# First row of attention units: the weights' conversion steps stand behind the copies in the iterations that multiply with the values

## The chip, the cores and the metric

The kernel runs on one core of one Trainium2 chip. The metric is the device time of one execution in microseconds (us); a kernel's time is the median of several executions. The engines are TensorE (PE, with its weight loads as PEld), VectorE (DVE), ScalarE (ACT), GpSimd (POOL) and SyncE (SP, which here only issues DMAs).

## What is computed

A thresholded attention over 8 batches and 8 heads (576 tokens, head size 64) is followed by a mixer block over tokens and channels. Cut to what matters:

```python
scores = q @ k.T / 8                          # (8, 8, 576, 576)
thresh = scores.max(-1) - tau
attn = exp(where(scores >= thresh, scores, -1e9) - scores.max(-1))
x = (attn / (attn.sum(-1) + 1e-9)) @ v        # heads side by side: (8, 576, 512)
h = relu(x.T @ w_tok1) @ w_tok2               # 576 -> 256 -> 576, per channel
u = x + h.T
out = u + relu(u @ w_ch1) @ w_ch2             # 512 -> 1536 -> 512
```

The four weights reach the kernel as 64-bit floats and have to be converted to 32 bits on the chip; q, k and v are 32-bit.

## The kernel before, in words

The attention is cut into 144 units of 128 score rows of two heads, 18 units per batch ("row"); a row has two groups of nine units, and one group covers two pairs of heads. A loop over u (line 640 on) is a software pipeline written out by hand: every engine does its instructions in the order in which the loop emits them, and nothing reorders them. For unit u the loop emits:

- scores(u): PE multiplies q with k into PSUM (L304), VectorE takes the row maxima mx (L309), POOL makes the bias from them (L310).
- values that are due (L411 and L416 on PE). In row 0 they come in the iterations u = 5, 8, 11, 14 and 17, which the code calls a visit. Their result pv lies in one of the two buffers of the PSUM pool ps_tr and is copied to xT by VectorE (L423); the copy is put into the list `copies` and emitted later in the same iteration.
- norm(u - 1): VectorE makes the reciprocals of the row sums (L333, L334), POOL multiplies e by them (L337).
- turn(u - 2): nine transposes on PE in three groups (L355); each group has a buffer of ps_tr, and its copy to eT (L357) is VectorE's for the first and the third group, ScalarE's for the second.
- weigh(u): ScalarE computes e by a Prelu from PSUM (L319), then the exponentials with their row sums (L326).
- on some iterations prep: VectorE transposes a loaded q and k (L286), at the end of the iteration before the one that uses them.

Between these lies the conversion of the weights, cut into 31 pieces with four raw buffers. weight(n) emits n steps, and three steps are one piece. Step k is part k mod 3 of piece k div 3. Every step has one VectorE instruction: L207 (part 0), L209 (part 1) and L213 (part 2). Part 0 also emits POOL's integer add that ends the piece before it (L221), and on SP the load of a later piece into the buffer that this add frees (L182); parts 1 and 2 also emit a ScalarE instruction for the next piece (L197 and L199). weight_to(x) goes on until int(x) steps are done. In row 0 an iteration without a visit brings the count to 2.25 (u - 1.5) in its middle and to 2.25 (u - 1) at its end (L706). An iteration with a visit does all of it in the middle, ahead of weigh, the copies and the turns. From row 1 on (u of 18 and above) other lines set the steps.

In row 0 the score tiles rotate over three PSUM buffers, from unit 18 on over two; the mixer's steps (L447 transposes, L454 and L464 token part, L507 and L528 channel part) then fill PE beside the attention of the next row. The channel steps need converted weights.

Of the kernel before, what the change touches and what calls it, by code (L numbers as in the profile page):

```python
# [21 lines left out]
def kernel(  # L22
# [206 lines left out]
    def weight(n):  # L229

        nonlocal steps_done
        for k in range(steps_done, min(steps_done + n, 3 * len(pieces) + 1)):
            i, part = divmod(k, 3)
            if part == 0:
                on_gpsimd(i - 1)
                if i:
                    load_piece(i - 1 + NRAW)
            else:
                on_scalar(i + 1, part - 1)
            on_vector(i, part)  # L240
            steps_done = k + 1

    def weight_to(x):

        weight(max(int(x) - steps_done, 0))
# [31 lines left out]
    def in_blocks(b):  # L277
        return b > 0
# [11 lines left out]
    def scores(u):  # L290
        b, p0, t = units[u]
        sc = [
            (ps_3rd if b == 0 and (2 * u + h) % 3 == 2 else ps_sc).tile([P, 2, MAIN], F32, tag="sc", name=f"sc{h}_{u}") for h in range(2)
        ]
        if t == SHARED:
            parts = [(b * NP + p0, slice(MAIN, S), slice(0, 64)), (b * NP + p0 + 1, slice(0, LAST), slice(64, P))]
        else:
            o = P * t if t < SHARED else LAST + P * (t - SHARED - 1)
            parts = [(b * NP + p0 + (t > SHARED), slice(o, o + P), slice(0, P))]
        order = [(f, part, h) for f in range(2) for part in parts for h in range(2)]  # L300
        for f, (n, cols, rows), h in order if b else sorted(order, key=lambda o: o[2]):
            r = slice(D * h, D * h + D)
            qT, kT = heads[n]
            nc.tensor.matmul(sc[h][rows, f, 0:HS], lhsT=qT[r, cols], rhs=kT[r, HS * f : HS * f + HS], start=True, stop=True)  # L304
        mx = small.tile([P, 2], F32, tag="mx", name=f"mx_{u}")
        bias = small.tile([P, 2], F32, tag="bias", name=f"bias_{u}")
        for h in range(2):
            c = slice(h, h + 1)
            nc.vector.tensor_reduce(out=mx[:, c], in_=sc[h][:, :, 0:HS], axis=AX.XY, op=ALU.max)  # L309
            nc.gpsimd.tensor_scalar(out=bias[:, c], in0=mx[:, c], scalar1=toff, scalar2=-SCALE, op0=ALU.add, op1=ALU.mult)  # L310
        st[u] = sc, bias

    def weigh(u):
        sc, bias = st.pop(u)
        rs = small.tile([P, 2], F32, tag="rs", name=f"rs_{u}")
        e = work.tile([P, 2 * S], F32, tag="e", bufs=3, name=f"e_{u}")
        for h in range(2):
            eh = e[:, S * h : S * h + S].rearrange("p (f x) -> p f x", f=2)
            nc.scalar.activation(out=eh, in_=sc[h][:, :, 0:HS], func=AF.Prelu, bias=bias[:, h : h + 1], scale=SCALE, alpha=STEEP)  # L319
        st[u] = e, rs  # L320

        if b_now:
            fill(0.2)
        for h in range(2):
            eh = e[:, S * h : S * h + S]
            nc.scalar.activation(out=eh, in_=eh, func=AF.Exp, bias=ntau, accum_out=rs[:, h : h + 1])  # L326
            if b_now:
                fill(0.2)

    def norm(u):  # L330
        e, rs = st[u]
        rr = small.tile([P, 2], F32, tag="rr", name=f"rr_{u}")
        nc.vector.tensor_scalar(out=rr, in0=rs, scalar1=1e-9, scalar2=None, op0=ALU.add)  # L333
        nc.vector.reciprocal(out=rr, in_=rr)  # L334
        for h in range(2):
            eh = e[:, S * h : S * h + S]
            nc.gpsimd.tensor_scalar(out=eh, in0=eh, scalar1=rr[:, h : h + 1], scalar2=1.0, op0=ALU.mult, op1=ALU.mult)  # L337
        st[u] = e
# [236 lines left out]
    def move_u():  # L575
        while moves:
            moves.popleft()()
# [10 lines left out]
    def fill(share):  # L588
        nonlocal credit
        credit += share * quota  # L590
        while todo and credit > 0:
            cost, step = todo.popleft()
            credit -= cost
            step()
        if not todo:
            credit = 0.0
# [4 lines left out]
    def push(b):  # L601
        nonlocal quota
        uT = xTs[b]
        steps, waits = token_mlp(b) if b else token_mlp(b, range(NP // 2, NP))
        old = list(todo)
        todo.clear()
        todo.extend(early)
        early.clear()

        for i, step in enumerate(steps):  # L610
            n = 2 if i in waits else 1
            todo.extend(old[:n] + [step])
            del old[:n]
        todo.extend(old)
        for i in range(2) if b % 2 == 0 else range(2, (2 * S + GR - 1) // GR):
            todo.extend(channel_mlp(b - b % 2, uT, i))
        quota = (sum(c for c, _ in todo) - (KEEP if b else KEEP_FIRST)) / (UB - 1)
# [11 lines left out]
    def values_due(u):  # L629
        while due and due[0][0] <= u:  # L630
            _, b, p0, g = due.popleft()
            values(b, p0, g)
            if b == 0 and p0 == 0 and g == 2:
                return True
            if p0 == NP - 2 and g == 2:
                if not in_blocks(b):
                    return True
                push(b)
        return False

    for u in range(len(units) + LAG + 4):
        on = u < len(units)
        if u == UB:
            late.close()
            ps_mm = ctx.enter_context(tc.tile_pool(name="ps_mm", bufs=2, space=bass.MemoryType.PSUM))
        if on:
            b_now, p0, t = units[u]
            n = b_now * NP + p0
        w = u - LAG
        back = 0 <= w < len(units)  # L650
        if on:
            scores(u)

        last = False
        visit = False
        if due and not in_blocks(due[0][1]):
            visit = due[0][0] <= u
            last = values_due(u)
        elif early:
            early.popleft()[1]()  # L660
        if 0 < u <= len(units):
            norm(u - 1)

        turns_left = b_now and back and not in_blocks(units[w][0])
        if b_now:
            if not turns_left:
                weight(2)
        else:


            weight_to(2.25 * (u - (1 if visit else 1.5)))
            if visit and on:
                weigh(u)
        while copies:
            copies.popleft()()
        if last and u < UB:
            early.extend(token_mlp(0, range(NP // 2))[0])
        elif last:
            push(0)
        if back:  # L680
            wb, wp, wt = units[w]
            if not in_blocks(wb):
                for i in range(3):
                    turn(w, i)
            if wt % GU == GU - 1:
                g = wt // GU
                if g < 2:
                    split_middle(wb * NP + wp + g)
                due.append((u + (2 if in_blocks(wb) else 1), wb, wp, g))
        if b_now:  # L690
            fill(0.4)
        if back and in_blocks(wb):
            turn_blocks(w)
        if b_now:
            weight(4 if turns_left else 2)
        if on and (b_now or not visit):
            weigh(u)
        elif b_now:
            fill(0.6)
        if b_now:  # L700
            weight(2)
        elif u == 0:
            on_scalar(0, 0)
            on_scalar(0, 1)
        else:
            weight_to(2.25 * (u - 1))  # L706
        if on:


            when = {3: (2, 0, 2), 4: (2, 2, 4), 5: (2, 4, 6), 6: (2, 6, 8), 8: (3, 0, 3), 0: (1, 3, 6), 1: (1, 6, 8)}  # L710
            if u == 0:
                load_qk(1, (nc.sync, nc.sync), range(0, 3))
            if t in when:
                m, lo, hi = when[t]
                if n + m < len(pairs):
                    load_qk(n + m, (nc.scalar if b_now else nc.sync,) * 2, range(lo, hi))
            if t in (3, 7) and n + 2 + t // 4 < len(pairs):
                load_v(n + 2 + t // 4)
            if t == 2:
                prep(n + 1)  # L720
            if t == 7 and n + 2 < len(pairs):
                prep(n + 2)
        if due and in_blocks(due[0][1]):
            values_due(u)

        if back and wt % GU == 0 or not on:
            move_u()
# [31 lines left out]
```

## Time and profile before

| | us |
|---|---|
| runs shown (4) | 1352.24, 1353.52, 1355.3, 1357.79 |
| median | 1354.41 |
| the profiled execution | 1352.24 |
| its span in the profile | 1350.5 |
| busy: PE / PEld / DVE / ACT / POOL | 1305.0 / 813.0 / 594.3 / 585.5 / 353.7 |

The costliest groups of the lines that the text speaks of, over the whole span (each line: code line, engine, operation, output and input, count, then busy time, mean ns of one, and the idle time before them with what ended most of it):

```profile
L309 DVE TENSOR_REDUCE mx<-sc 128x1 f32<-128x576 f32 x288 | 204.3, 750 | 445.5 <-PE sc L304 445.3
L319 ACT ACTIVATE e<-sc,bias 128x576 f32<-128x576 f32 x288 | 200.0, 740 | 182.6 <-POOL bias L310 177.5
L337 POOL TENSOR_SCALAR e<-e,rr 128x576 f32<-128x576 f32 x288 | 214.7, 758 | 14.3 <-ACT g L508 2.6
```

In a timeline line the first number is the start in us from the start of the span, the second the time taken, then engine, line, operation and tiles; what stands in square brackets is the idle time of the engine just before, and what ended it. Instructions of one line that follow each other are merged, with their number behind the x. The page's slices give the busy share of each fortieth of the span (33.8 us) in tenths; 9 is 90% or more.

### The profile page before, as it was taken

Reading aid. Unit: us, or ns where it says so; the run is one execution under the profiler, and the core shown is the slowest. Engines: PE = TensorE matmul, PEld = TensorE weight load, DVE = VectorE, ACT = ScalarE, POOL = GpSimd, SP = SyncE. Lnnn points to the kernel's source line nnn. Section 1 sums busy time; section 2 is a strip of 40 time slices with the busy share of each in tenths; the row PEclk is TensorE's granted clock in tenths of the full one; section 3 lists DMA queues with packets and bytes.
Section 4 is the critical chain, followed back from the end, with each engine's and each line's share of the span. In section 5 each row is a group of like instructions: output and inputs, shape, how many; then the busy total and the mean of one; then the engine's idle time right before and its main releaser. Section 6 shows DMA issues by size and latency. Waiting matters only on the chain.

```text
span 1350.5 us, 17840 instructions
## 1 busy us (share of the span) xinstructions
PE 1305.0 (97%) x6162; PEld 813.0 (60%) x6162; DVE 594.3 (44%) x1026; ACT 585.5 (43%) x1299; POOL 353.7 (26%) x683
## 2 busy tenths in 40 slices
PE   6888899999999999999999999999999999999999
PEld 4555656547474666655665567565656566575677
DVE  6878874445443434434334445434443454201000
ACT  6776654445445435443434444354333454120110
POOL 4565652222222213222222222222221222100000
PEclk9999999999999999999999999999999999999999
DMA  5434764535353544543345435534443453400000
GB/s 123 119 89 122 204 169 99 129 93 131 88 136 82 119 105 97 128 106 88 87 107 128 97 85 125 122 82 114 111 102 84 114 117 78 113 23 17 23 24 32
DMA packets 296746, 135.31 MB, mean 100 GB/s; under 512 B 204816, under 2 KB 289552, under 8 KB 296656
## 3 DMA queue, kind: packets, MB, share of 16 engines
q1 hardware_dynamic: 168048, 118.16, 34.3%
q10 hardware_dynamic: 128608, 16.01, 7.5%
q8 instruction: 49, 0.80, 0.2%
q14 instruction: 41, 0.34, 0.1%
HBM read 43.25 MB, written 9.44 MB: 39 GB/s over the span
## 4 chain that ended last, share of the span: by engine, by line
PE 84%; DVE 6%; ACT 3%; DMA 2%; SPq 2%; POOL 1%; issue 1%; ACTq 0%; DVEq 0%; POOLq 0%
PE c L528 25%; PE c L507 25%; PE sc L304 11%; PE pv L416 8%; PE t L454 5%; PE t L464 4%; PE pv L411 3%; DVE mx L309 2%; SPq L376 2%; PE tx L447 1%; ACT e L319 1%; DMA lk<-in_k_dram 1%; PE tr L355 1%; DMA scratch<-in_moe_w_ch_dram 1%; PE c_h L555 1%
## 5 line engine op out<-in xcount | busy, mean ns | idle before, releaser
L507 PE MATMUL c<-xT,wc 128*128 128x256 f32 (+1 forms) x1920 | 400.8, 362 | 0.1
L309 DVE TENSOR_REDUCE mx<-sc 128x1 f32<-128x576 f32 x288 | 204.3, 750 | 445.5 <-PE sc L304 445.3
L528 PE MATMUL c<-wc,g 128*128 128x512 f32 x840 | 379.0, 597 | 0.0
L507 PEld LDWEIGHTS c<-xT,wc 128*128 128x128 f32 x1920 | 335.0, 191 | 69.6 <-issue 29.7
L310 POOL TENSOR_SCALAR bias<-mx,toff 128x1 f32<-128x1 f32 x288 | 82.3, 286 | 777.0 <-DVE mx L309 721.0
L319 ACT ACTIVATE e<-sc,bias 128x576 f32<-128x576 f32 x288 | 200.0, 740 | 182.6 <-POOL bias L310 177.5
L528 PEld LDWEIGHTS c<-wc,g 128*128 128x128 f32 x840 | 154.4, 190 | 176.3 <-issue 173.4
L326 ACT ACTIVATE e<-e,ntau 128x576 f32<-128x576 f32 x288 | 221.1, 771 | 0.0
L337 POOL TENSOR_SCALAR e<-e,rr 128x576 f32<-128x576 f32 x288 | 214.7, 758 | 14.3 <-ACT g L508 2.6
L508 ACT ACTIVATE g<-c 128x256 f32<-128x256 f32 (+1 forms) x240 | 87.1, 363 | 296.5 <-PE c L507 275.8
L304 PE MATMUL sc<-kT,qT 64*128 64x288 f32 (+1 forms) x1280 | 194.2, 437 | 11.4 <-DVE kT L286 6.8
L367 DVE STREAM_TRANSPOSE T<-e 128x1152 f32<-128x1152 f32 x126 | 171.9, 1365 | 4.7 <-DMA eT<-T 2.4
L304 PEld LDWEIGHTS sc<-kT,qT 64*128 64x128 f32 (+1 forms) x1280 | 107.8, 180 | 98.0 <-issue 57.5
L416 PE MATMUL pv<-eT,lv 128*64 128x384 f32 (+1 forms) x1024 | 136.2, 406 | 0.0
L416 PEld LDWEIGHTS pv<-eT,lv 128*64 128x64 f32 x1024 | 75.3, 137 | 49.3 <-issue 41.3
L421 ACT COPY xT<-pv 128x384 f32<-128x384 f32 (+1 forms) x56 | 21.0, 401 | 164.4 <-PE pv L416 162.4
L464 PE MATMUL t<-w,a 128*128 128x288 f32 x256 | 74.6, 417 | 8.7 <-DVE xT L468 5.3
L540 DVE TENSOR_TENSOR us<-c,ut 128x512 f32<-128x512 f32 x26 | 17.9, 690 | 137.5 <-PE c L528 124.6
L454 PE MATMUL t<-x_sb,w 128*128 128x512 f32 (+1 forms) x180 | 73.3, 555 | 0.0
L464 PEld LDWEIGHTS t<-w,a 128*128 128x128 f32 x256 | 45.3, 190 | 30.9 <-issue 10.5
L468 DVE TENSOR_TENSOR xT<-xT,t 128x288 f32<-128x288 f32 x64 | 28.2, 446 | 70.0 <-PE t L464 69.4
L326 ACT ACTIVATION_READ_ACCUMULATOR e<-e,ntau 128x1 f32 x288 | 56.6, 197 | 0.0
(49 smaller groups left out, 563.3 us busy)
## 6 DMA issues: line engine op xcount, KB each, us to landing
eT<-T SPq DMA_DIRECT2D x672, 108.0 KB, 2.3
scratch<-in_moe_w_ch_dram SPq DMA_DIRECT2D x24, 512.0 KB, 3.8
lv<-in_v_dram SPq DMA_DIRECT2D x32, 288.0 KB, 3.2
out_dram<-us SPq DMA_DIRECT2D x35, 256.0 KB, 2.2
lk<-in_k_dram ACTq DMA_DIRECT2D x111, 72.0 KB, 2.6
lq<-in_q_dram ACTq DMA_DIRECT2D x106, 72.0 KB, 2.3
ut<-us SPq DMA_DIRECT2D x192, 32.0 KB, 1.9
lq<-in_q_dram SPq DMA_DIRECT2D x18, 72.0 KB, 3.3
```

Of the source, the lines that this page charges most:

```text
L304: nc.tensor.matmul(sc[h][rows, f, 0:HS], lhsT=qT[r, cols], rhs=kT[r, HS * f : HS * f + HS], start=True, stop=True)
L309: nc.vector.tensor_reduce(out=mx[:, c], in_=sc[h][:, :, 0:HS], axis=AX.XY, op=ALU.max)
L319: nc.scalar.activation(out=eh, in_=sc[h][:, :, 0:HS], func=AF.Prelu, bias=bias[:, h : h + 1], scale=SCALE, alpha=STEEP)
L326: nc.scalar.activation(out=eh, in_=eh, func=AF.Exp, bias=ntau, accum_out=rs[:, h : h + 1])
L337: nc.gpsimd.tensor_scalar(out=eh, in0=eh, scalar1=rr[:, h : h + 1], scalar2=1.0, op0=ALU.mult, op1=ALU.mult)
L367: nc.vector.transpose(out=T[:, :, place, :].rearrange("p a (c x) -> p c a x", c=NK), in_=e.rearrange("p (c a x) -> p c a x", c=NK, a=4))
L416: nc.tensor.matmul(to[r], lhsT=lv[:, j, :], rhs=e[j], start=False, stop=(c == NI - 1), skip_group_check=True)
L454: nc.tensor.matmul(to, lhsT=w1[:, t, P * m : P * m + P], rhs=x_sb[:, t, cols], start=(t == 0), stop=(t == NT - 1))
L464: nc.tensor.matmul(to, lhsT=a[:, m, P * c : P * c + P], rhs=w2[:, m, HS * f : HS * f + HS], start=(m == 0), stop=(m == NTK - 1))
L507: nc.tensor.matmul(ps, lhsT=wc1[:, j, c, :], rhs=uT[:, c, GR * i : GR * i + n], start=(c == 0), stop=(c == NCC - 1))
L508: nc.scalar.activation(out=s["g"][:, j, 0:n], in_=ps, func=AF.Relu)
L528: nc.tensor.matmul(flat, lhsT=s["g"][:, j, P * t : P * t + P], rhs=wc2[:, j, :], start=(j == 0 and b > 0), stop=(j == NJ - 1), skip_group_ ...
```

## The change

In iterations with a visit, weigh(u) is emitted where the conversion steps were, and the steps are left to the line at the end of the iteration (L706 before, L707 after), which brings the count to the same 2.25 (u - 1). Iterations without a visit are as before. Twelve steps move: 6 to 8 at u = 5, 13 and 14 at u = 8, 20 and 21 at u = 11, 27 and 28 at u = 14, and 33 to 35 at u = 17.

```diff
         else:
-            weight_to(2.25 * (u - (1 if visit else 1.5)))
-            if visit and on:
+            if visit:
                 weigh(u)
+            else:
+                weight_to(2.25 * (u - 1.5))
         while copies:
             copies.popleft()()
```

Engine by engine, in the five iterations: on VectorE, the conversions stood between norm(u - 1) and the copy xT, and stand behind the last eT copy, ahead of prep where there is one. On ScalarE, L197 and L199 stood ahead of e(u), and stand behind the eT copy. The orders on PE, POOL and SP are the same in both kernels.

## The prediction

> **What bounds the kernel now.** First the page's slices: which engine is full, and where.
>
> ```profile
> PE   6888899999999999999999999999999999999999
> DVE  6878874445443434434334445434443454201000
> ```
>
> From about the sixth slice on TensorE is full to the end. The change touches only iterations u = 5, 8, 11, 14 and 17, that is up to some 105 us, where neither engine is full. Busy time by stretch (us, then PE, PEld, DVE, ACT, POOL; last columns granted clock, DMA share, GB/s):
>
> ```profile
> 0.00:105.00 105.00, 82.89 (x490) 53.09 (x491) 76.95 (x167) 74.62 (x157) 59.60 (x106) 0.98 0.48 111
> 105.00:190.00 85.00, 75.74 (x366) 49.32 (x365) 76.61 (x122) 58.05 (x120) 51.35 (x64) 0.96 0.63 165
> ```
>
> In the first stretch no engine is over 79%: the time is a chain that goes round between engines. The chain of waits passes there through VectorE's mx, the PE's turns and VectorE's copies. What the change does to the start of mx(u+1), VectorE's first work for the next unit, is therefore what it does to the end: everything behind it keeps its order, and from 190 us on a full PE only starts earlier or later. So I read VectorE's timeline around each of the five visits, and beside it PE and POOL. The last visit, u = 17 (start, duration, instruction, idle time before it):
>
> ```profile
> 94.97 0.17 DVE L334 RECIPROCAL rr<-rr 128x2 f32<-128x2 f32 x1
> 95.05 0.41 DVE L207 TENSOR_SCALAR high<-high 128x512 f32<-128x512 f32 x1
> 95.49 0.44 DVE L209 TENSOR_SCALAR wc<-high 128x512 uint32<-128x512 uint32 x1
> 95.96 1.03 DVE L213 SCALAR_TENSOR_TENSOR wc<-scratch,wc 128x512 uint32<-128x512 uint32 x1
> 96.92 0.61 DVE L423 COPY xT<-pv 128x192 f32<-128x192 f32 x2
> 97.45 0.54 DVE L357 COPY eT<-tr 128x384 f32<-128x384 f32 x1
> 98.63 0.56 DVE L357 COPY eT<-tr 128x384 f32<-128x384 f32 x1 [0.64 <-PE tr L355]
> 100.55 1.42 DVE L309 TENSOR_REDUCE mx<-sc 128x1 f32<-128x576 f32 x2 [1.36 <-PE sc L304]
> ```
>
> and TensorE beside it:
>
> ```profile
> 93.57 1.47 PE L416 MATMUL pv<-eT,lv 128*64 128x192 f32 x16
> 94.97 0.55 PE L355 MATMUL tr<-ident,e 128*128 128x128 f32 x3
> 97.67 0.92 PE L355 MATMUL tr<-ident,e 128*128 128x128 f32 x6 [2.15 <-DVE xT L423]
> 98.52 1.93 PE L304 MATMUL sc<-kT,qT 64*128 64x288 f32 x8
> ```
>
> The values pv are ready at 93.57 + 1.47 = 95.04, but their copy xT starts at 96.92, behind three conversions; the second turn needs pv's buffer, so PE stands still 2.15 us. Here the change can gain. At u = 11 the same instructions stand in a gap that is there anyway:
>
> ```profile
> 61.17 0.42 DVE L207 TENSOR_SCALAR high<-high 128x512 f32<-128x512 f32 x1
> 62.35 0.56 DVE L423 COPY xT<-pv 128x384 f32<-128x384 f32 x1 [0.76 <-PE pv L416]
> 64.02 0.56 DVE L357 COPY eT<-tr 128x384 f32<-128x384 f32 x1 [0.64 <-PE tr L355]
> 64.49 0.77 DVE L286 STREAM_TRANSPOSE qT<-lq 128x576 f32<-128x576 f32 x1
> 65.84 1.38 DVE L309 TENSOR_REDUCE mx<-sc 128x1 f32<-128x576 f32 x2
> ```
>
> xT waits 0.76 us for pv after the conversions; but behind the last eT copy VectorE goes on without a gap through the transposes to mx. Moved there, they cost.
>
> **The change part by part.** Nothing is added or removed: 12 VectorE conversions (3, 2, 2, 2, 3) and 8 ScalarE conversions move behind the copies. PE's, POOL's and SP's orders stay as they are: the four integer adds L221 and the four weight loads behind them pass nothing on their queues. The step costs are those from one start to the next. For each visit, the shift of mx(u+1):
>
> u = 5: xT waits for pv until 34.28 after the conversions, so nothing is gained. The last eT copy starts at 35.96 and frees VectorE 0.48 later, at 36.44; L207 0.30, L209 0.34 and L213 about 0.36 (its 0.77 here ran beside POOL's L337; the 128x288 form took 0.44) end at 37.44, and mx now starts at 37.19 after 0.68 of idle time: **+0.25**. Bounds: 0 and, with L213 held as now, +0.66.
>
> u = 8: pv ends at 46.34 + 1.47 = 47.81; elsewhere xT starts 0.04 behind it, so at 47.85 instead of 48.35: -0.50. Turns and scores follow, mx(9) could start at 50.80; the conversions (0.71) run from 50.05 to 50.76 and are just covered: **-0.50**. Bounds: -0.71 (no wait for pv) and 0.
>
> u = 11: L213 0.36 and L207 0.34 now stand in front of the transposes: **+0.70**. L207 needs ScalarE's L199, which moves too, behind ScalarE's eT copy (63.79): some 0.37 for the copy and 0.55 for itself, done by about 64.7, in time for 64.85. VectorE's next idle time, 0.80 us at 73.05, doesn't give it back: bias(12) and so e(12) come later, the turns behind them by some 0.58, and L209 then waits behind POOL's L221, which is 0.70 later. Bounds: 0 and +0.8. POOL's add for piece 6 now waits for L213 and comes some 2 us later, and so does the load behind it on SP (63.73) with two q/k loads and a v load; piece 10 is first read at 76.21 and the pair at u = 16, so nothing waits.
>
> u = 14: pv ends at 79.13, long after the conversions (77.94). Behind the last eT copy (81.31) they take 0.44 + 0.36 and end at 82.11, where mx(15) starts at 82.08: **+0.03**.
>
> u = 17: xT starts at 95.08, 1.84 sooner. The turns, the eT copies and sc(18) follow 1.84 sooner, the last copy is over at 97.27. There POOL decides, and this is the disputed cost. How conversions fare beside POOL shows at u = 13:
>
> ```profile
> 73.24 1.29 POOL L221 TENSOR_TENSOR wc<-wc,scratch 128x512 int32<-128x512 int32 x1
> 73.53 1.29 DVE L209 TENSOR_SCALAR wc<-high 128x512 uint32<-128x512 uint32 x1
> ```
>
> L209, 0.44 us alone, ended 0.29 us after L221 did. At u = 17 POOL's L337 (95.47, now 2.13 beside the conversions, 1.47 where undisturbed) ends at about 96.94 and L221 runs from there to 98.2. L207 then ends at 98.55, L209 and L213 at 99.6: mx(18) comes 0.95 sooner, not 1.84. But in u = 18 VectorE stands idle 1.88 us before its eT copy (104.13, waiting for PE), and PE is the full 1.84 sooner; there the rest returns until L207 meets POOL's next L221 (102.44 - 0.95 + 1.47 = 102.96 to 104.25). L209 starts at 104.6 where it started at 106.25: **-1.65**. Bounds: -0.95 (nothing returns) and -1.84 (POOL holds nothing).
>
> The Trainium skill's page "SBUF — State Buffer", section "SBUF: two separate sides", says that VectorE's two-port or two-input instructions and GpSimd take turns on one port pair, held for a whole instruction; it speaks against this place, and would give the -0.95 at mx(18) by itself.
>
> A second thing hangs on PE's standstill: the clock (columns as above).
>
> ```profile
> 95.54:98.95 3.41, 1.28 (x10) 1.00 (x12) 2.74 (x6) 2.73 (x6) 3.33 (x3) 1.00 0.00 0
> 98.95:102.36 3.41, 3.41 (x13) 2.16 (x10) 1.90 (x5) 0.00 (x0) 0.54 (x2) 0.50 0.71 186
> ```
>
> PE was busy 1.28 of 3.41 us in the first line, and in the second the clock is half. There are three such stretches of 3.41 us between 95 and 190 us, each behind one with at most 1.45 us of busy PE. Here it slows sc(18) and ten L454 matmuls (3.38 us; 2.43 at u = 16). If PE stands idle less at u = 17, it may stay fast: at most 3.41 / 2 = 1.7 us of PE time. I count nothing for it, since VectorE and POOL set L209's start above without it. "TensorE: Matmul & The Clock Gate", section "HAM oscillation", gives gaps over about 3.4 us as what drops the clock; the 2.15 us gap here would then be harmless, and a changed clock no part of the sum.
>
> ScalarE: e(u) is let go earlier by one or two conversions, but at u = 8, 14 and 17 it waits for bias on POOL anyway, and at u = 5 and 11 nobody is waiting for it. Behind eT the conversions fall into ScalarE's waits for PE (1.42 to 5.09 us long at the next turn): nothing.
>
> Sum: 0.25 - 0.50 + 0.70 + 0.03 - 1.65 = **-1.17 us**. The profiled execution spans 1350.5 and took 1352.24 (1.74 around it): 1349.33 + 1.74 = 1351.07. The median of the runs shown lies 2.17 above that execution: 1354.41 - 1.17 = **1353.2 us**.
>
> **Rivals.**
> 1. The gain of u = 17 is not passed on: bounds of the visits 5 to 14 remain, +0.48, so 1354.9. For it: SP's queue and weight loads stand in the chain of waits from 141 us on. Against: those loads start behind L221, which moves with the rest.
> 2. Slower by POOL: at the four other visits, too, a conversion at the iteration's end is held by a POOL instruction as at 73.53, 1.29 - 0.44 = 0.85 us each, 3.4 in all: 1353.2 + 3.4 = 1356.6. It decides where POOL is still busy when the last eT copy ends. Against: it is idle there at all four (35.2 to 38.1, 49.7 to 52.2, 63.7 to 66.7, 80.5 to 82.9).
> 3. The clock: one half-speed stretch fewer on the path, 1353.2 - 1.7 = 1351.5. For it: the window above. Against: VectorE and POOL bind behind it.
>
> **How the numbers follow.** Forecast 0.55, rival 1 0.20, rival 2 0.10, rival 3 0.15. The range takes in all three rivals, widened for the scatter of a median (the single runs lie 2.2 below to 3.4 above theirs): 1350.0 to 1357.0. A measurement of this kernel tells about 0.3%, 4.1 us, from no change: faster needs under 1350.3, rival 3 with u = 8 and 17 at their best, 0.08; slower needs over 1358.5, rival 2 with nothing gained at u = 17, 0.06; within, 0.86.
>
> **What would show it.** Right: xT at u = 17 directly behind pv and PE's 2.15 us gap down to about 0.3; L207 there longer than 0.41 us beside L221; mx(12) 0.7 us later against the visit before; no idle time before mx at u = 5, 8 and 14; a start of unit 18's mx about 0.5 us earlier and of unit 19's about 1.2 us earlier in the span. Wrong: new idle time before the transposes at u = 16 (a late load), conversions of over 1 us at several visits, or a shift at 190 us that differs from that at 110 us.

## The result, and the profile after

The changed kernel takes 1352.4 us (median of 41 runs, 1349.91 to 1356.35) beside 1354.23 of the kernel before (64 runs on the same chips, 1350.44 to 1359.16). The ratio is 0.9987, with a 95% interval of 0.9982 to 0.9993: 1.8 us less (2.4 to 0.9), and 1353.2 was forecast. The profiled execution of after took 1351.4 us and spans 1349.6.

The page's slices and the two stretches of after, to be laid beside those of before:

```profile
PE   6888899999999999999999999999999999999999
DVE  5889874445443435434334445434443454201000
```

```profile
0.00:105.00 105.00, 84.07 (x491) 54.20 (x491) 77.25 (x170) 76.50 (x159) 56.52 (x106) 0.97 0.48 110
105.00:190.00 85.00, 75.59 (x361) 48.62 (x363) 75.04 (x120) 56.46 (x118) 52.94 (x64) 0.96 0.62 165
```

Little has changed at this scale: PE is busy 84.07 us for 82.89 in the first stretch and 75.59 for 75.74 in the second, and the mean clock is much the same. The change has to be read visit by visit. VectorE of after at u = 17 and in u = 18:

```profile
97.11 0.62 DVE L423 COPY xT<-pv 128x192 f32<-128x192 f32 x2 [0.34 <-PE pv L416]
97.65 0.55 DVE L357 COPY eT<-tr 128x384 f32<-128x384 f32 x1
98.84 0.56 DVE L357 COPY eT<-tr 128x384 f32<-128x384 f32 x1 [0.64 <-PE tr L355]
99.31 0.68 DVE L207 TENSOR_SCALAR high<-high 128x512 f32<-128x512 f32 x1
100.03 0.43 DVE L209 TENSOR_SCALAR wc<-high 128x512 uint32<-128x512 uint32 x1
100.48 0.69 DVE L213 SCALAR_TENSOR_TENSOR wc<-scratch,wc 128x512 uint32<-128x512 uint32 x1
101.09 1.42 DVE L309 TENSOR_REDUCE mx<-sc 128x1 f32<-128x576 f32 x2
...
104.82 1.40 DVE L209 TENSOR_SCALAR wc<-high 128x512 uint32<-128x512 uint32 x1
```

TensorE of after beside it:

```profile
95.60 1.47 PE L416 MATMUL pv<-eT,lv 128*64 128x192 f32 x16
97.00 0.55 PE L355 MATMUL tr<-ident,e 128*128 128x128 f32 x3
97.88 0.92 PE L355 MATMUL tr<-ident,e 128*128 128x128 f32 x6 [0.34 <-DVE xT L423]
98.73 1.24 PE L304 MATMUL sc<-kT,qT 64*128 64x288 f32 x8
99.90 2.43 PE L454 MATMUL t<-x_sb,w 128*128 128x256 f32 x10
```

and POOL:

```profile
96.97 1.48 POOL L337 TENSOR_SCALAR e<-e,rr 128x576 f32<-128x576 f32 x2
98.40 1.30 POOL L221 TENSOR_TENSOR wc<-wc,scratch 128x512 int32<-128x512 int32 x1
...
104.42 1.51 POOL L221 TENSOR_TENSOR wc<-wc,scratch 128x512 int32<-128x512 int32 x1
```

xT starts 0.04 us behind pv, and PE's gap is 0.34 where it was 2.15. L207 takes 0.68 instead of 0.41: L221 ends at 99.70 and L207 at 99.99, 0.29 later, the distance the forecast used. But two rows of PE also changed that the change does not touch: sc(18) took 1.24 where it was 1.93, and the ten L454 took 2.43 where they were 3.38. The half-speed clock is gone from there. In before, the L454 and the wait of VectorE behind them were:

```profile
100.38 3.38 PE L454 MATMUL t<-x_sb,w 128*128 128x256 f32 x10
104.13 0.56 DVE L357 COPY eT<-tr 128x384 f32<-128x384 f32 x1 [1.88 <-PE tr L355]
```

To separate the two I measured, in every trace, the time from the start of one unit's mx to that of the next. At the five visits, where no half-speed stretch falls in and nothing near was edited, this interval repeats between executions mostly to 0.02 us, while whole runs of one kernel scatter by 6 us and more. Where VectorE waits for a load it repeats less well: u = 7 takes 5.40 to 5.91 us over all the profiles. In the table, a visit's column is from mx(u) to mx(u+1), "17-19" is from mx(17) to mx(19), "5-19" from mx(5) to mx(19); * marks an interval lengthened by a half-speed stretch. The time against before is the ratio, with its interval, times the median of before on the same chip.

| moved visits, other edits | u=5 | u=8 | u=11 | u=14 | 17-19 | 5-19 | time against before, us |
|---|---|---|---|---|---|---|---|
| none (before) | 6.90 | 5.23 | 6.62 | 6.62 | 16.34* | 79.53 | |
| none, again | 6.90 | 5.23 | 6.62 | 6.62 | 16.29* | 79.77 | one run |
| none, PE kept busy at 17 | 6.90 | 5.24 | 6.63 | 6.62 | 14.88 | 78.09 | +0.5 (-1.5 to +2.4) |
| 5, 8, 11, 14 | 7.12 | 4.55 | 7.33 | 7.18* | 14.88 | 78.54 | -1.1 (-3.3 to +1.1) |
| 17 | 6.90 | 5.23 | 6.62 | 6.62 | 14.21 | 77.81 | -2.7 (-4.6 to -0.8) |
| 8, 17 | 6.90 | 4.53 | 6.66 | 6.69* | 14.21 | 77.01 | -1.5 (-3.4 to +0.4) |
| 8, 17, ahead of the last copy | 6.90 | 4.51 | 6.62 | 6.62 | 14.18 | 77.16 | -1.9 (-3.4 to -0.5) |
| 8, 17, PE kept busier | 6.90 | 4.51 | 6.63 | 6.62 | 14.23 | 76.88 | -3.4 (-5.4 to -1.4) |
| all (after) | 7.13 | 6.30* | 7.33 | 6.53 | 14.24 | 79.10 | -1.8 (-2.4 to -0.9) |
| all, again | 7.11 | 5.99* | 7.33 | 6.54 | 14.23 | 79.11 | one run |
| all, PE kept busier | 7.11 | 4.51 | 8.92* | 6.66 | 14.46 | 79.27 | -2.4 (-4.1 to -0.7) |

### The profile page after: what moved, and what is told of

Its sections match the earlier page's. It is cut to its first block, busy times and chain, and to the rows that moved or that the text cites. A ratio compares the mean times of both kernels' runs of the same rounds, so it can differ in the third digit from the quotient of the medians.

```text
span 1349.6 us, 17839 instructions
## 1 busy us (share of the span) xinstructions
PE 1305.4 (97%) x6162; PEld 812.6 (60%) x6162; DVE 593.0 (44%) x1026; ACT 586.0 (43%) x1299; POOL 352.2 (26%) x683
## 4 chain that ended last, share of the span: by engine, by line
PE 87%; DVE 5%; DMA 2%; ACT 2%; SPq 1%; POOL 1%; issue 1%; ACTq 0%; DVEq 0%; POOLq 0%
PE c L528 27%; PE c L507 25%; PE sc L304 11%; PE pv L416 9%; PE t L454 5%; PE t L464 4%; PE pv L411 3%; DVE mx L309 2%; PE tx L447 1%; SPq L376 1%; PE tr L355 1%; DMA scratch<-in_moe_w_ch_dram 1%; ACT e L319 1%; DMA lk<-in_k_dram 1%; PE c_h L555 1%
## 5 line engine op out<-in xcount | busy, mean ns | idle before, releaser
L337 POOL TENSOR_SCALAR e<-e,rr 128x576 f32<-128x576 f32 x288 | 213.1, 753 | 14.7 <-ACT g L508 2.6
L454 PE MATMUL t<-x_sb,w 128*128 128x512 f32 (+1 forms) x180 | 72.4, 549 | 0.0
```

Source lines behind the costliest of these rows:

```text
L454: nc.tensor.matmul(to, lhsT=w1[:, t, P * m : P * m + P], rhs=x_sb[:, t, cols], start=(t == 0), stop=(t == NT - 1))
```

## The experiments

My theory after the result: at u = 17 the larger part of what was gained is the clock, and the copies themselves gave less than forecast. The rival is the forecast's: the copies gave all of it. The edits are against the kernel before unless something else is said.

**Which visits gave it.** Two kernels move one set of visits each:

```diff
-            weight_to(2.25 * (u - (1 if visit else 1.5)))
+            if u not in (17,):        # second kernel: (5, 8, 11, 14)
+                weight_to(2.25 * (u - (1 if visit else 1.5)))
```

> Only the conversions of u = 17 stand behind the copies; u = 5, 8, 11 and 14 are as in the kernel before. Theory (the terms of the prediction add up, and u = 17 carries the gain): the start of unit 19's mx (109.82 us before) moves to 108.2 us, and the time falls by 1.65 us, by 2.1 us if the profile after is taken (its shift there from unit 17's mx to unit 19's). Rival (the gain of u = 17 is given back behind unit 19): mx of unit 19 earlier, but the time within 0.5 us of the kernel before.

> The conversions of u = 5, 8, 11 and 14 stand behind the copies, those of u = 17 ahead of them as in the kernel before. Theory: the small terms add up to +0.48 us, unit 17's mx (93.48 us before) starts at 94.0 us, and the time is 0.5 us above the kernel before. Rival (the gain of the change is made in the other visits and u = 17 matters little): the time falls by 1 us or more.

The times (-2.7 and -1.1 us) overlap widely. The intervals do not: with u = 17 alone, 17-19 is 14.21. But with the other four moved and u = 17 as before, it is 14.88, where before has 16.34. PE there, in the second kernel:

```profile
98.62 0.92 PE L355 MATMUL tr<-ident,e 128*128 128x128 f32 x6 [1.69 <-DVE xT L423]
99.47 1.24 PE L304 MATMUL sc<-kT,qT 64*128 64x288 f32 x8
100.64 2.42 PE L454 MATMUL t<-x_sb,w 128*128 128x256 f32 x10
```

PE stood still for 1.69 us, and the clock stayed full. So the old order costs 14.88 under a full clock and 16.3 under the half one.

**The two visits that were forecast to gain.** The same edit with the set (8, 17):

> Only the two visits where xT waits for VectorE and not for pv (u = 8 and 17) have their conversions behind the copies. Theory: -0.50 and -1.65 without the +0.25, +0.70 and +0.03 of the others, so 2.15 us below the kernel before and about 1 us below the kernel after; unit 12's mx at 65.3 us, unit 19's at 107.7 us. Rival (each visit's shift is lost at the next wait for a load, such as that before the transposes at u = 16): no faster than e1_only17.

5-19 is 77.01, 2.5 us under before and 2.1 under after; the time, -1.5 (-3.4 to +0.4), shows neither a gain over before nor one over after.

**The clock by itself.** No conversion is moved; the first group of transposes at u = 17 is done five times, so that PE works while it waits for xT (the repeats write the same values):

```diff
-        for c in range(3):
+        for c in [0, 1, 2] * (5 if (u, third) == (15, 0) else 1):
```

> The kernel before, in which the first transpose group of u = 17 is done five times over (12 extra transposes, about 2 us) so that PE is busy where it stood idle 2.15 us. Nothing else moves. Theory (VectorE and POOL set the pace behind u = 17, the clock adds nothing): sc of unit 18 and the ten L454 matmuls run at full clock (1.25 and 2.43 us instead of 1.93 and 3.38), but the time changes by less than 0.5 us. Rival (the clock is what the change gains at u = 17): unit 19's mx comes 1.4 to 1.7 us earlier and the time falls as much, although no conversion was moved.

Its PE timeline:

```profile
96.36 1.86 PE L355 MATMUL tr<-ident,e 128*128 128x128 f32 x15
98.98 0.92 PE L355 MATMUL tr<-ident,e 128*128 128x128 f32 x6 [0.77 <-DVE xT L423]
99.84 1.24 PE L304 MATMUL sc<-kT,qT 64*128 64x288 f32 x8
101.01 2.42 PE L454 MATMUL t<-x_sb,w 128*128 128x256 f32 x10
```

sc(18) and L454 are fast, and 17-19 is 14.88, the same as in the second kernel: 1.46 us of the 2.10 come without moving anything. The end, however, shows no gain (+0.5, -1.5 to +2.4); a gain of the full 1.46 lies only just inside the interval. In this profile a half-speed stretch of 6.8 us came at 107.1, and from mx(19) to mx(26) it took 62.88 us where the two profiles of before took 61.62 and 63.92: whether the 1.46 was given back there, they do not show.

**Does time lost at u = 17 reach the end?** L209 of one piece is done nine times there (it overwrites its output with the same values); the line added stands around L209:

```diff
+                for _ in range(9 if i == 11 else 1):
```

> The kernel before, with VectorE's L209 of piece 11 done nine times instead of once, ahead of the copy xT of u = 17: about 3.6 us more VectorE work there (0.44 us each), the same values. It asks whether a delay at u = 17 reaches the end. Theory (row 0 is one chain, and PE behind it is full): unit 18's mx and unit 19's mx start about 3.6 us later, and the time rises by 3 to 4 us. Rival (row 1 has slack that takes in a shift): unit 19's mx 3.6 us later, the time up by less than 1.8 us; then the forecast's gain of 1.65 us at u = 17 could not be the time's.

17-19 is 21.60, 5.26 us over before, and the time +7.4 us (5.4 to 9.6). What is lost here arrives at the end in full (the rest may be half-speed stretches: two, at 59 and 76 us, lengthen u = 11 and u = 14 by 1.57 and 0.39 us in this profile, ahead of the edit; another, at 103.5 us, lies inside 17-19, as one does in before). This does not show that a gain arrives too: the delay also pushes back the next L221 (to 113.50) and the load behind it, which rival 1 holds to set the pace. The size was off: the nine took 5.86 us, not nine times 0.44, beside POOL's two L337 (99.08, 1.86) and L221 (100.91, 1.44). In this kernel the lines L209 and L213 are L210 and L214:

```profile
99.09 5.86 DVE L210 TENSOR_SCALAR wc<-high 128x512 uint32<-128x512 uint32 x9
104.98 0.69 DVE L214 SCALAR_TENSOR_TENSOR wc<-scratch,wc 128x512 uint32<-128x512 uint32 x1
```

**A better place?** At u = 8 and 17, the same set as above, the conversions stand between the two eT copies, in VectorE's 0.64 us of waiting for the transposes:

```diff
                 for i in range(3):
+                    if i == 2 and u in (8, 17):
+                        weight_to(2.25 * (u - 1))
```

> Conversions of u = 8 and 17 between the first and the last eT copy of the visit, where VectorE waits 0.64 us for PE in both kernels; those of u = 5, 11 and 14 stay where the kernel before has them, in the wait for pv. Theory: of the 1.5 us at u = 17 some 0.6 more is covered than behind the last copy; from unit 17's mx to unit 19's 13.5 to 13.9 us (14.2 in the kernel after), at u = 8 as e3_8_and_17; the time 2 us or more below the kernel before. Rival (POOL's L337, which runs just then, holds L207 and L209, and the last eT copy comes later): 14.2 us or more from unit 17's mx to unit 19's.

17-19 is 14.18 against 14.21 behind the last copy: nothing is won. VectorE and POOL of this kernel show why:

```profile
95.83 0.42 DVE L207 TENSOR_SCALAR high<-high 128x512 f32<-128x512 f32 x1
96.28 0.78 DVE L209 TENSOR_SCALAR wc<-high 128x512 uint32<-128x512 uint32 x1
97.09 1.67 DVE L213 SCALAR_TENSOR_TENSOR wc<-scratch,wc 128x512 uint32<-128x512 uint32 x1
98.67 0.55 DVE L357 COPY eT<-tr 128x384 f32<-128x384 f32 x1
```

```profile
95.06 1.72 POOL L337 TENSOR_SCALAR e<-e,rr 128x576 f32<-128x576 f32 x2
96.74 1.46 POOL L221 TENSOR_TENSOR wc<-wc,scratch 128x512 int32<-128x512 int32 x1
```

L213, 0.69 alone, took 1.67 beside L221. If it is the add that holds it, putting the add off to u = 18 must move the hold with it (the edit is against the kernel just shown):

```diff
-                on_gpsimd(i - 1)
-                if i:
-                    load_piece(i - 1 + NRAW)
+                for j in {11: (), 12: (10, 11)}.get(i, (i - 1,)):
+                    on_gpsimd(j)
+                    if j >= 0:
+                        load_piece(j + NRAW)
```

> e6_between_8_17 with POOL's add of piece 10 (L221) and the load behind it put off from u = 17 to u = 18. In e6 L213 took 1.67 us beside that add instead of 0.69, and u = 17 was no shorter than with the conversions behind the copies (5.94 us from mx to mx). Theory (a POOL instruction holds VectorE's conversions until it ends): L213 of u = 17 back at 0.69 us, 5.0 us at u = 17, and the hold comes back at u = 18, where two adds follow each other (9 us or more instead of 8.25). Rival (L213 was long for another reason, PE's or ScalarE's): 1.6 us again at u = 17.

At u = 17 L213 takes 0.69 again and mx(17) to mx(18) falls from 5.94 to 5.17; mx(18) to mx(19) rises from 8.25 to 9.46, where POOL now does both adds (103.45, 2.72) and VectorE has

```profile
103.87 1.15 DVE L207 TENSOR_SCALAR high<-high 128x512 f32<-128x512 f32 x1
105.06 1.40 DVE L209 TENSOR_SCALAR wc<-high 128x512 uint32<-128x512 uint32 x1
```

The hold goes where the add goes. A half-speed stretch at 106.1 us lies in this interval too, but VectorE has no idle time from 103.39 to mx(19) at 109.59, so it is not what lengthens it. Together it is 14.62, worse than 14.18.

**Both kernels profiled once more**, since a half-speed stretch had come at u = 8 in after:

> The kernel before once more, for another profile: does PE's clock drop behind the standstill of u = 17 in every execution? Theory (the clock's 3.41 us windows lie at another phase in each execution, so the standstill of 2.15 us trips it in some only): either a stretch at half clock from 98 to 103 us and 16.3 us from unit 17's mx to unit 19's, or none there and 14.9 us. Rival (the standstill always trips it, and e2_all_but_17 escaped because its own was 1.69 us): 16.3 us.

> The kernel after once more, for another profile. Theory: from unit 17's mx to unit 19's 14.2 us at full clock again, since PE's standstill there is only 0.34 us; the local costs at u = 5 and 11 again 0.2 and 0.7 us against the kernel before; at u = 8 6.3 us from mx to mx if the clock drops there again, 4.5 us if not. Rival (the times from mx to mx differ from one execution to the next by as much as they differ between the kernels): 15 us or more at u = 17, or no cost at u = 11.

Both repeat: 16.29 at u = 17 in before, and in after a stretch again at u = 8 (44.1 us, 5.99). So the half-speed stretch at u = 17 came in both profiles of before, and the one at u = 8 in both of after. The latter, in the first profile of after, stretch by stretch, with u = 17 below (us, then PE, PEld, DVE, ACT, POOL; clock, DMA share, GB/s):

```profile
40.00:43.41 3.41, 2.06 (x15) 1.26 (x13) 3.38 (x9) 3.41 (x10) 2.85 (x6) 1.00 0.25 54
43.41:46.83 3.42, 3.42 (x16) 2.36 (x17) 3.01 (x5) 2.02 (x5) 2.23 (x5) 0.50 0.37 78
95.27:98.69 3.42, 3.08 (x33) 2.22 (x27) 2.56 (x7) 2.38 (x5) 2.26 (x5) 1.00 0.00 0
98.69:102.10 3.41, 3.41 (x20) 2.65 (x19) 3.19 (x6) 2.02 (x5) 1.17 (x2) 1.00 0.34 95
```

PE was busy 2.06 us of the first line and half as fast in the second; at u = 17 it is now busy 3.08 of 3.42 and stays fast.

**Against these stretches**, more repeated transposes, once on the kernel with 8 and 17 moved, once on after:

```diff
-        for c in range(3):
+        for c in [0, 1, 2] * {(5, 1): 2, (11, 0): 3}.get((u, third), 1):
```

> e3_8_and_17 with nine extra transposes that repeat a group while PE would wait for ScalarE: one extra group (0.49 us) in the middle of turn(5), two in the first of turn(11). In the traces so far PE's clock dropped for 3.41 us behind windows of 40 to 43 us and 71 to 74 us in which PE was busy 1.5 to 2.1 us. Theory (PE's standing still within one window drops the clock, and that hits the path in some executions): no stretch at half clock before 100 us, 6.90, 4.53, 6.62 and 6.62 us from mx to mx at u = 5, 8, 11 and 14, and the time 1 us or more below the kernel after. Rival (the extra transposes delay the copies behind them): u = 7 or u = 13 longer by 0.3 us or more, and no gain.

> The kernel after with the same extra transposes. Both profiles of the kernel after had a stretch at half clock from 43 or 44 us, over the values of u = 8 (6.30 and 5.99 us from mx to mx there, against 4.53 to 4.55 where all conversions of u = 8 stood behind the copies at full clock). Theory: no such stretch, 4.53 us at u = 8, still 7.12 and 7.33 us at u = 5 and 11; unit 17's mx about 1.7 us earlier than in the kernel after (93.4 us), and the time falls by up to as much. Rival (the longer u = 8 comes from the change's conversions and not from the clock): 6.0 us or more at u = 8 again.

On after, the stretch at 43 us is gone and u = 8 takes 4.51, with the same conversions in the same place: it was the clock, and not they, that made 6.30 of it. But another stretch falls at 59.3 us, where none was, and u = 11 takes 8.92: 5-19 is no shorter (79.27). The windows of the clock lie differently in each execution, so one profile does not show that the transposes took the one stretch away or brought the other. On the kernel with 8 and 17 moved, no stretch is left between 30 us and 109 us, 5-19 is the shortest of all (76.88), and the time, -3.4 us (-5.4 to -1.4; ratio 0.9975, 0.996 to 0.999), is the best against its own before. Its interval overlaps those of the others, so it is not shown to beat after.

## Why the prediction was right, and where it was not

The forecast of -1.17 us lies within the measured -1.8 (-2.4 to -0.9). The terms show that this was in part luck. At full clock they are:

- u = 5, +0.25: +0.22. No idle time before mx, as said.
- u = 8, -0.50: -0.70 (4.53 for 5.23), the bound without a wait. In both profiles of after the term was +0.8 to +1.1 all the same, by a half-speed stretch on sc(8) and the first values of the visit; no term of the sum had that.
- u = 11, +0.70: +0.71. The conversions stand bare ahead of the transposes:

```profile
65.35 0.56 DVE L357 COPY eT<-tr 128x384 f32<-128x384 f32 x1 [0.64 <-PE tr L355]
65.82 0.45 DVE L213 SCALAR_TENSOR_TENSOR w<-scratch,w 128x288 uint32<-128x288 uint32 x1
66.19 0.42 DVE L207 TENSOR_SCALAR high<-high 128x512 f32<-128x512 f32 x1
66.52 0.77 DVE L286 STREAM_TRANSPOSE qT<-lq 128x576 f32<-128x576 f32 x1
```

- u = 14, +0.03: +0.04 where no half-speed stretch lies near (6.66 in "all, PE kept busier"). In after it is 6.53 and 6.54, but a stretch from 74 us makes the interval before it longer, 5.80 and 5.79 for 5.68; the two together are 0.03 longer than in before.
- u = 17, -1.65: -2.10 against before as profiled, but only -0.64 against the old order under a full clock (14.24 for 14.88; -0.67 with u = 17 moved alone). **This is the step that failed**: "I count nothing for it, since VectorE and POOL set L209's start above without it". In before, PE's clock did set it: VectorE waited 1.36 us for sc(18) and 1.88 for the next turn, and sc(18) and L454 were 0.69 and 0.95 us too long. With the clock full, those waits are 0.68 and 0.92 in the second kernel, and they are all that the moved copies can take away before VectorE itself binds:

```profile
100.81 1.42 DVE L309 TENSOR_REDUCE mx<-sc 128x1 f32<-128x576 f32 x2 [0.68 <-PE sc L304]
103.43 0.56 DVE L357 COPY eT<-tr 128x384 f32<-128x384 f32 x1 [0.92 <-PE tr L355]
...
105.11 0.60 DVE L207 TENSOR_SCALAR high<-high 128x512 f32<-128x512 f32 x1
105.74 0.43 DVE L209 TENSOR_SCALAR wc<-high 128x512 uint32<-128x512 uint32 x1
```

PE's gap shrinks by 1.35 us (1.69 to 0.34), but the three conversions now stand on VectorE's path between the last copy and mx(18) for 1.78 us (99.31 to 101.09): 0.41 is left at mx(18) (5.98 for 6.39) and another 0.23 at mx(19) (8.27 for 8.50). In u = 18 L207 of after starts 1.02 us sooner behind mx(18) (3.28 for 4.30), but L209 is then held beside L221, 1.40 for 0.43, which takes nearly all of it. Even the 0.23 hangs on which of the two engines starts first: in after L207 starts 0.05 ahead of L221 (104.37, 104.42), while in "all, PE kept busier", with the same order there, it starts 0.16 behind it, is held itself, and mx(18) to mx(19) is 8.50 again:

```profile
106.16 1.29 POOL L221 TENSOR_TENSOR wc<-wc,scratch 128x512 int32<-128x512 int32 x1
106.32 1.42 DVE L207 TENSOR_SCALAR high<-high 128x512 f32<-128x512 f32 x1
```

So 1.46 us of the 2.1 at u = 17 came from the clock, which was rival 3's mechanism, and the forecast gave it to the copies. At full clock throughout, the five terms sum to 0.22 - 0.70 + 0.71 + 0.04 - 0.64 = -0.37 us. As profiled they are 0.23 + 1.07 + 0.71 - 0.09 - 2.10 = -0.18 us, and -0.46 in the second pair of profiles: what the clock gave at u = 17 was lost again at u = 8, where the half-speed stretch costs 1.77 (6.30 for 4.53). So three errors of opposite signs meet in the forecast's -1.17: 1.46 of clock not counted at u = 17, 1.01 too much for the copies there, and the stretch at u = 8. The measured 1352.4 lies midway between the forecast's 1353.2 and rival 3's 1351.5.

5-19 fell by a little more, by 0.43 (79.53 to 79.10). The largest change outside the visits stands at u = 16, where the forecast saw none: mx(16) to mx(17) takes 6.83 to 7.02 us in the four profiles with the conversions of u = 5, 8, 11 and 14 moved, and 7.21 to 7.53 in the nine others. VectorE waits there for a load ahead of the transposes, 1.26 us in before and 0.88 in after:

```profile
92.11 0.78 DVE L286 STREAM_TRANSPOSE qT<-lq 128x576 f32<-128x576 f32 x1 [1.26 <-DMA lv<-in_v_dram]
93.76 0.78 DVE L286 STREAM_TRANSPOSE qT<-lq 128x576 f32<-128x576 f32 x1 [0.88 <-DMA lq<-in_q_dram]
```

Why this wait is shorter was not traced.

Of the signs that the forecast named, those at single instructions came: xT behind pv, the gap of 0.34, the longer L207, mx(12) 0.7 later, no idle time before mx at u = 5, 8 and 14. Those in the span did not. Unit 18's mx is 0.54 us later (101.09 for 100.55) and unit 19's 0.46 earlier, where 0.5 and 1.2 earlier were forecast. And the shift at 190 us differs from that at 110, which was to be a sign of being wrong: against before it is -0.46 at mx(19), -1.38 at mx(26), +0.18 at mx(29) (190 us) and -0.9 at the end of the span, and in the second pair of profiles -0.40, -3.64, -2.86 and -4.4. The step "What the change does to the start of mx(u+1) ... is therefore what it does to the end" is not shown for shifts as small as these.

The POOL hold was in the right place: at u = 17 and in u = 18, L207 0.68 for 0.41 and L209 1.40 for 0.43. Rival 2 fell: at the four other visits no moved conversion took over 0.46. Rival 1, 1354.9, is above the measured time, and with u = 17 moved alone the time fell by 2.7 us (4.6 to 0.8); the delay that arrived in full fits, but would not have refuted it alone.

"The Trainium skill", page "TensorE: Matmul & The Clock Gate", section "HAM oscillation", gives gaps over about 3.4 us as what slows the clock; here the measurement decides against it as a bound, since gaps of 2.15 and 2.23 us were followed by a half-speed stretch in the two profiles of before. "SBUF — State Buffer", section "SBUF: two separate sides", has VectorE's instructions with two inputs wait while a GpSimd instruction holds the port pair that they share; L213, which has two, agrees (1.67 beside L221, 0.69 alone).

What stays open: both profiles of after are only 0.4 to 0.7 us ahead of before from mx(5) to mx(19), against 1.8 measured. So the cause of most of the 1.8 us at the end is not shown. The other 1 us or so must come elsewhere, and differs by execution: from mx(19) to mx(26) the profiles of before took 61.62 and 63.92, those of after 60.70 and 60.68, and behind that the order wanders by a microsecond or two with half-speed stretches (at 161 to 164 and at 248 us in some) and with jumps that I did not trace. Whether the stretch at u = 8 comes in every execution of after, and that at u = 17 in every one of before, two profiles of each cannot say. And the medians, good to about 2 us in the experiments, can't tell the terms apart; only the intervals do, and each rests on one or two profiles.

## What to carry to other kernels

When work is moved out of an engine's wait, look at what the wait did to the clock as well as to the queue behind it: here the clock was two thirds of the local gain, and in both profiles of after a like loss stood at another visit. Give a gain its full size only up to where the moved work itself becomes the path; behind the last copy, three conversions took back 0.9 of the 1.35 us that PE had won. For edits far below the scatter of whole runs, compare the intervals between marks of the program (here mx to mx) instead of medians, and mark those with a half-speed stretch in them. They tell what an edit does in its place, and not yet what of it reaches the end.

## What was not expected of the hardware

- The granted clock drops on a fixed grid of 3.41 us in each execution. In the thirteen traces laid on it, from 30 to 260 us, a window at full clock with PE busy 1.43 us or less always had a half-speed stretch behind it, one of over 2.1 us never; between, both came. With 2.06 us it dropped in after (40.00 to 43.41) and not in before (40.91 to 44.32). Once dropped, it stayed down for a second window in five traces although PE was busy 2.5 us or more in the first. At u = 17 standstills of 2.15 and 2.23 us were followed by a drop in the two profiles of before, and one of 1.69 was not in the kernel with 5, 8, 11 and 14 moved; as the grid lies differently in each execution, neither is a bound.
- Nine L209 in a row beside three POOL instructions (two L337, one L221) took 5.86 us, where nine times the 0.44 that one takes alone would be 4.0.
